# The first token tile's result goes out whole: a gated mix of a state-space convolution and a spatial-shift MLP on one core

## The chip, the cores and the metric

The kernel runs on one core of a Trainium2 chip. A core has five engines that run their own instruction lists side by side and wait for one another through semaphores: TensorE (PE; its weight loads are listed as PEld), VectorE (DVE), ScalarE (ACT), GpSimd (POOL) and SyncE (SP), which in this kernel issues nearly all DMA transfers. The metric is the device time of one execution in microseconds (us), as the median of several runs. Lower is better.

## The reference

The input `x` has 2048 tokens of 448 channels. Two branches are computed from it and mixed with a gate per token:

```python
g = sigmoid((x * gate_w).sum(-1, keepdims=True))
a = ssm_conv(x)            # long convolution per channel, plus x * D_skip
h = gelu(layernorm(x) @ w1)
hs = shift(h) @ w2         # quarters of the channels shifted by +1, -1, +2, -2 tokens
x1 = x + hs
b = x1 + gelu(layernorm(x1) @ w3) @ w4     # 448 -> 1792 -> 448
out = g * a + (1 - g) * b
```

All of it is float32.

## The kernel before

**Tiling.** The 2048 tokens are worked on in `NB` = 4 blocks of `TB` = 512, each of `NT` = 4 token tiles of 128. Tile `q` = 4 * block + place runs from 0 to 15. The tile `xs` holds the tokens in SBUF, 128 to a tile, and is overwritten in steps until it holds the result.

**Stages.** `units` lists 72 pieces of matmul work: the spatial-shift layer of all blocks, four pieces each, and then the channel MLP, 14 pieces a block. `first` (line 478) makes the hidden layer of a piece, `second` (line 602) adds its product with the second weight to the accumulators of the block's four token tiles. Float32 operands are split into a high and a low part, so each product is three matmuls. Around this, VectorE and ScalarE run the convolution branch as scans (`ssm_scan`, line 757), and SP moves turned tiles through DRAM (`xd`, `xr`, `yd`, `ysb`).

**Writing the result.** A token tile is finished when both branches have been added to it: `residual` (line 615) adds the MLP, `ssm_out` (line 787) the convolution. Each calls `done`, and the second call issues the result's transfer on SP (line 579). In block 0, tiles 0 to 3, the transfer goes out as two halves of 64 tokens each; in the other blocks as one of 128. The very last tile is written by `last_two` in two column pieces, of 320 and 128 channels (line 643).

**Lanes.** The framework that builds the program gives the transfers in turn to eight lanes, that is eight semaphores, DMAHW0 to DMAHW7; the next transfer takes the next lane, and after lane 7 comes lane 0. A transfer waits, where it isn't known already, until the one before it on its lane has landed. An instruction that needs a transfer's data waits on that transfer's lane.

**The end.** After the mixer the kernel reads a flag (line 59) and branches on it (line 60, `tc.If(ok == 0)`). With these inputs the body, `general_convolution`, is skipped. On the skipping path SP waits for its transfers, lane by lane from 0 to 7, with one wait instruction for each lane; these eight have line 60. At the program's end (line 1297) it waits once more for each lane together with one other semaphore, and then all engines meet in a barrier. The order of SP's list is that of the code as it is written; no scheduler moves it.

Of the kernel before, what the change touches and what calls it, by code (L numbers as in the profile page):

```python
# [22 lines left out]
NT = TB // 128  # L23
# [156 lines left out]
def mixer_and_small_steps(ctx, tc, xs, gg, okm, x, xT, xb, x0, w1, w2, w3, w4, gate, par, logdt, dskip, ident, out):  # L180
# [392 lines left out]
    def done(b, j):  # L573
        q = NT * b + j
        parts[q] = parts.get(q, 0) + 1
        if parts[q] == 2:
            for p in range(0, 128, 64 if b == 0 else 128):
                t = slice(p, p + (64 if b == 0 else 128))
                nc.sync.dma_start(out[q * 128 + t.start:q * 128 + t.stop], xs[t, q, :])

    ADDED = {}
# [26 lines left out]
    def residual(n, j):  # L608
        kind, b, i = units[n]
        q = NT * b + j  # L610
        r = xs[:, q, :]
        if kind == "a":
            nc.vector.tensor_add(r, ACC[j], r)
        else:
            nc.vector.scalar_tensor_tensor(r, ACC[j], gs[:, q:q + 1], r, op0=OP.mult, op1=OP.add)
            done(b, j)


    def last_two():

        n = len(units) - 2
        last = NT * NB - 1

        def add(acc, q, c):
            r = xs[:, q, c]
            nc.vector.scalar_tensor_tensor(r, acc, gs[:, q:q + 1], r, op0=OP.mult, op1=OP.add)  # L626

        add(ACC[NT - 1], last, slice(0, D))
        for j in range(NT):
            t = slice(j * 128, (j + 1) * 128)  # L630
            q = NT * (NB - 1) + j
            for c in (slice(0, D),) if q < last else (slice(0, D - 128), slice(D - 128, D)):
                acc = ACC[j] if q < last else ps.tile([128, c.stop - c.start], F32, name="p1", tag="p1", bufs=3)
                for m in (n, n + 1):
                    wh, wl = W4[units[m][2]]
                    for p in range(3):
                        nc.tensor.matmul(acc, (UL if p == 2 else UH)[m][:, t], (wl if p == 1 else wh)[:, c],  # L637
                                         start=q == last and m == n and p == 0, stop=m > n and p == 2)
                add(acc, q, c)
                if q < last:  # L640
                    done(NB - 1, j)
                else:
                    nc.sync.dma_start(out[q * 128:(q + 1) * 128, c], xs[:, q, c])
# [140 lines left out]
    def ssm_out(b, i):  # L784
        j = NT * b + i
        r = xs[:, j, :]
        nc.vector.scalar_tensor_tensor(r, YS.pop((b, i)), gg[:, j:j + 1], r, op0=OP.mult, op1=OP.add)
        done(b, i)
# [395 lines left out]
    for b in range(NB):  # L1184
        s0 = (7, 18, 31, 46)[b]
        for i in range(NT):
# [5 lines left out]
            q, when = n + (4 if b in (1, 2) else 3), late if b == 3 else before  # L1192
# [108 lines left out]
```

## Time and profile before

| what | us |
|---|---|
| median of 3 runs | 372.56 |
| lowest and highest | 371.94, 372.81 |
| profiled execution, its own time | 371.42 |
| span of that execution, first to last instruction | 369.6 |

The profile is that of one execution, whose time stands in the third row. The span is the part between its first and its last instruction, and the rest lies around it. In rows of the profile, "L579" is line 579 of the kernel, `out<-in` are the program's names, and an engine's name with a q (SPq) is its sequencer, which issues transfers, waits and branches. Times of such rows are starts from the span's beginning; durations are in ns. The closing part of the program holds these pieces of SP, by the views of their lines:

| piece | line | start, us |
|---|---|---|
| last three whole tiles issued | 579 | 361.8 to 364.3 |
| last tile's two column pieces issued | 643 | 365.0, 365.5 |
| branch | 60 | 365.9 |
| waits for the eight lanes | 60 | 367.7 to 368.2 |
| waits of the program's end | 1297 | 368.3 to 369.6 |

### The profile page before, as it was taken

What the parts mean: (1) busy time and instruction counts of PE and PEld (TensorE: products, weight loads), DVE (VectorE), ACT (ScalarE), POOL (GpSimd) and SP (SyncE); (2) the same over time, 40 slices, a digit from 0 to 9 for tenths busy, and PEclk for the clock granted to TensorE, in tenths of its full rate; (3) what the DMA queues carried; (4) which work ended last, traced back from release to release, by engine and by line L of the source; (5) the groups of instructions that cost most, each with busy time, mean ns of one, the idle gap of its engine ahead of it and who ended that gap; (6) DMA issues with size and microseconds to landing.
All of it is one profiled execution on the core that took longest, in us unless ns stands there. A gap on an engine that the chain in (4) does not pass through costs nothing.

```text
span 369.6 us, 5310 instructions
## 1 busy us (share of the span) xinstructions
PE 363.9 (98%) x1734; PEld 314.8 (85%) x1734; DVE 308.5 (83%) x571; ACT 216.1 (58%) x383; POOL 63.8 (17%) x176
## 2 busy tenths in 40 slices
PE   8999999999999999999999999999999999999995
PEld 5988888888888888888888888888888888888884
DVE  4999979788989997388789899997889999999433
ACT  5887678776674737944373774554656745445220
POOL 1000433000400000110014333324234324000000
PEclk9999999999999999999999999999999999999998
DMA  7994116727938064001833514367485611361213
GB/s 268 394 398 143 48 54 128 160 82 254 381 122 192 2 121 150 0 0 51 192 93 82 84 28 121 86 178 126 86 127 114 177 27 25 72 178 30 66 48 105
DMA packets 88495, 46.14 MB, mean 125 GB/s; under 512 B 67216, under 2 KB 82960, under 8 KB 87824
## 3 DMA queue, kind: packets, MB, share of 16 engines
q1 hardware_dynamic: 88032, 45.27, 45.5%
q10 hardware_dynamic: 432, 0.49, 0.4%
q8 instruction: 15, 0.25, 0.3%
q14 instruction: 16, 0.13, 0.1%
HBM read 34.74 MB, written 11.01 MB: 124 GB/s over the span
## 4 chain that ended last, share of the span: by engine, by line
PE 95%; DMA 3%; SPq 0%; ACT 0%; DVE 0%; issue 0%
PE p L478 48%; PE acc L602 45%; DMA raw<-x_in 2%; DMA w1r<-w_in 1%; PE acc L637 1%; PE misc L363 0%; PE p L637 0%; SPq L246 0%; ACT xh L955 0%; SPq L264 0%; DVE xs L626 0%; PE misc L734 0%
## 5 line engine op out<-in xcount | busy, mean ns | idle before, releaser
L539 ACT ACTIVATE uf<-p 128x512 f32<-128x512 f32 x56 | 33.5, 599 | 113.3 <-PE p L478 113.3
L478 PE MATMUL p<-xh,w3l 128*128 128x512 f32 x224 | 70.1, 394 | 0.0
L478 PE MATMUL p<-xh,w3h 128*128 128x512 f32 x224 | 70.0, 394 | 0.0
L757 DVE TENSOR_TENSOR_SCAN z<-z,carry 128x512 f32<-128x512 f32 x48 | 61.6, 1283 | 4.2 <-POOL z L751 0.5
L602 PE MATMUL acc<-w4l,uh 128*128 128x448 f32 x216 | 56.3, 366 | 0.0
L602 PE MATMUL acc<-w4h,uh 128*128 128x448 f32 x216 | 56.0, 365 | 0.0
L602 PE MATMUL acc<-w4h,ul 128*128 128x448 f32 x216 | 55.8, 364 | 0.0
L569 DVE TENSOR_TENSOR ul<-uf,uh 128x512 fp32r<-128x512 f32 x56 | 38.1, 681 | 20.0 <-ACT uh L549 19.8
L478 PEld LDWEIGHTS p<-xh,w3l 128*128 128x128 f32 x224 | 42.1, 188 | 9.8
L478 PEld LDWEIGHTS p<-xh,w3h 128*128 128x128 f32 x224 | 42.1, 188 | 6.6
L478 PE MATMUL p<-xl,w3h 128*128 128x512 f32 x168 | 47.7, 392 | 0.0
L602 PEld LDWEIGHTS acc<-w4h,uh 128*128 128x128 f32 x216 | 40.5, 188 | 6.0
L602 PEld LDWEIGHTS acc<-w4h,ul 128*128 128x128 f32 x216 | 40.6, 188 | 3.6
L602 PEld LDWEIGHTS acc<-w4l,uh 128*128 128x128 f32 x216 | 40.5, 188 | 3.4
L752 ACT ACTIVATE z<-zs,nu 128x512 f32<-128x512 f32 x64 | 42.3, 710 | 0.2 <-DVE xl L409 0.2
L478 PEld LDWEIGHTS p<-xl,w3h 128*128 128x128 f32 x168 | 31.5, 188 | 7.2
L549 ACT ACTIVATE uh<-uf 128x512 fp32r<-128x512 f32 x56 | 35.4, 633 | 1.8
L751 POOL COPY z<-carry 128x1 f32<-128x1 f32 x48 | 32.7, 692 | 16.0 <-DVE zs L763 15.9
L759 POOL COPY carry<-z 128x1 f32<-128x1 f32 x48 | 13.1, 273 | 105.1 <-DVE z L757 104.4
L344 POOL TENSOR_TENSOR t<-r 128x4 f32<-128x4 f32 (+1 forms) x5 | 3.1, 626 | 117.4 <-DVE r L343 117.4
L757 DVE TENSOR_TENSOR_SCAN z<-z,carry,zero 128x512 f32<-128x512 f32 x16 | 20.0, 1248 | 0.0
L602 PE MATMUL acc<-w2l,uh 128*128 128x448 f32 x64 | 19.9, 367 | 0.0
(207 smaller groups left out, 543.7 us busy)
## 6 DMA issues: line engine op xcount, KB each, us to landing
zs<-xT_in SPq DMA_DIRECT2D x4, 1024.0 KB, 8.1
yd<-yt SPq DMA_DIRECT2D x56, 64.0 KB, 2.0
ysb<-yd SPq DMA_DIRECT2D x16, 224.0 KB, 2.7
raw<-xb_in SPq DMA_DIRECT2D x3, 1032.0 KB, 12.6
raw<-w_in SPq DMA_DIRECT2D x3, 1024.0 KB, 5.6
xd<-xt SPq DMA_DIRECT2D x16, 192.0 KB, 2.1
xr<-xd SPq DMA_DIRECT2D x16, 192.0 KB, 3.1
raw<-w_in SPq DMA_DIRECT2D x3, 896.0 KB, 4.6
```

Of the source, the lines that this page charges most:

```text
L344: eng.tensor_mul(t, y, y)
L478: nc.tensor.matmul(p[:, t0:t1], (wl if w else wh)[:, k, :], (xl if x_ else xh)[:, k, o + t0:o + t1], start=(q == 0 and fresh), stop=stop i ...
L539: nc.scalar.activation(UF[n], P1[n], AF.Gelu_apprx_tanh)
L549: nc.scalar.activation(UH[n], UF[n], AF.Copy)
L569: nc.vector.tensor_sub(UL[n], uf, f32(UH[n]))
L602: nc.tensor.matmul(ACC[j], (UL if p == 2 else UH)[n][:, t], wl if p == 1 else wh, start=first_, stop=last_)
L637: nc.tensor.matmul(acc, (UL if p == 2 else UH)[m][:, t], (wl if p == 1 else wh)[:, c], start=q == last and m == n and p == 0, stop=m > n a ...
L751: nc.gpsimd.tensor_copy(z4[:, m, 0:1], carry[:, k, m:m + 1])
L752: nc.scalar.activation(z4[:, m, 1:], ZS[b][:, k, :], AF.Copy, scale=nu[:, k, m:m + 1])
L757: nc.vector.tensor_tensor_scan(z, z, up, carry[:, k, m:m + 1], OP.add, OP.add)
L759: nc.gpsimd.tensor_copy(carry[:, k, m:m + 1], z[:, TB - 1:])
```

## The change

The width of a half is now chosen by the tile's number instead of by the block. Tile 0 goes out as one transfer of 128 tokens; tiles 1 to 3 still go out in halves; all others are as they were.

```diff
         if parts[q] == 2:
-            for p in range(0, 128, 64 if b == 0 else 128):
-                t = slice(p, p + (64 if b == 0 else 128))
+            h = 64 if 0 < q < NT else 128
+            for p in range(0, 128, h):
+                t = slice(p, p + h)
                 nc.sync.dma_start(out[q * 128 + t.start:q * 128 + t.stop], xs[t, q, :])
```

One line is added, so lines behind it have a number higher by one in the changed kernel: L580 for L579, L644 for L643, L1298 for L1297.

SP's list, where the first results go out. Ahead of these rows stand two loads of `ysb`; `out_dram` is the output, "64x448" the piece, and the brackets name the semaphores that SP waits for ahead of the transfer. Before:

```order
L579 DMA out_dram<-xs 64x448 x2
L579 DMA out_dram<-xs 64x448 [waits DMAHW7_49]
L579 DMA out_dram<-xs 64x448 [waits DMAHW0_49]
L579 DMA out_dram<-xs 64x448 [waits DMAHW1_49,DVE_49]
L579 DMA out_dram<-xs 64x448 [waits DMAHW2_49]
L579 DMA out_dram<-xs 64x448 [waits DMAHW3_49,DVE_49]
L579 DMA out_dram<-xs 64x448 [waits DMAHW4_49]
L432 DMA xd<-xt 128x3x128 [waits DMAHW5_49,DVE_49]
L434 DMA xd<-xt 128x64 [waits DMAHW6_49]
```

And now, the same place:

```order
L580 DMA out_dram<-xs 128x448
L580 DMA out_dram<-xs 64x448
L580 DMA out_dram<-xs 64x448 [waits DMAHW7_49]
L580 DMA out_dram<-xs 64x448 [waits DMAHW0_49,DVE_49]
L580 DMA out_dram<-xs 64x448 [waits DMAHW1_49]
L580 DMA out_dram<-xs 64x448 [waits DMAHW2_49,DVE_49]
L580 DMA out_dram<-xs 64x448 [waits DMAHW3_49]
L432 DMA xd<-xt 128x3x128 [waits DMAHW4_49,DVE_49]
L434 DMA xd<-xt 128x64 [waits DMAHW5_49]
```

Eight transfers have become seven, the first of them whole, and from the `xd` rows on each transfer stands on the lane below the one it had.

The end of SP's list on the path that is taken. The first row's wait tells its own lane, and from there the transfers can be counted on: one lane further each. Before:

```order
L775 DMA yd<-yt 32x16x32 [waits DMAHW7_49]
L782 DMA ysb<-yd 128x448 [waits DMAHW5_49,DMAHW4_49,DMAHW6_49,DMAHW3_49,DMAHW7_49,DMAHW2_49,DMAHW0_49]
L782 DMA ysb<-yd 128x448 [waits DMAHW1_49]
L782 DMA ysb<-yd 128x448 [waits DMAHW0_49,DVE_49]
L782 DMA ysb<-yd 128x448 [waits DMAHW1_49,DVE_49]
L579 DMA out_dram<-xs 128x448 [waits DVE_49] x3
L643 DMA out_dram<-xs 128x320 [waits DVE_49]
L643 DMA out_dram<-xs 128x128 [waits DVE_49]
L60 COMPARE_AND_BRANCH
```

And now:

```order
L776 DMA yd<-yt 32x16x32 [waits DMAHW6_49]
L783 DMA ysb<-yd 128x448 [waits DMAHW5_49,DMAHW4_49,DMAHW6_49,DMAHW3_49,DMAHW7_49,DMAHW2_49,DMAHW1_49]
L783 DMA ysb<-yd 128x448 [waits DMAHW0_49]
L783 DMA ysb<-yd 128x448 [waits DMAHW7_49,DVE_49]
L783 DMA ysb<-yd 128x448 [waits DMAHW0_49,DVE_49]
L580 DMA out_dram<-xs 128x448 [waits DVE_49] x3
L644 DMA out_dram<-xs 128x320 [waits DVE_49]
L644 DMA out_dram<-xs 128x128 [waits DVE_49]
L60 COMPARE_AND_BRANCH
```

Before, the `yd` row is on lane 7, the four `ysb` rows on lanes 0 to 3, the three whole results on 4 to 6, and the two pieces of the last tile on 7 and 0. Now they are on 6, on 7 and 0 to 2, on 3 to 5, and on 6 and 7. Behind the branch, the path that is taken holds the eight waits, in this order both before and now:

```order
L60 UNCONDITIONAL_BRANCH [waits DMAHW0_49,DMAHW1_49,DMAHW2_49,DMAHW3_49,DMAHW4_49,DMAHW5_49,DMAHW6_49,DMAHW7_49]
```

The order of the instructions of the other four engines is the same as before; some of their waits name the lane below.

## The prediction

> **What bounds the kernel now.** I read the views from the coarse to the fine: the page, then the stretches, then the last five microseconds instruction by instruction. The page first.
>
> ```profile
> span 369.6 us, 5310 instructions
> PE 363.9 (98%) x1734; PEld 314.8 (85%) x1734; DVE 308.5 (83%) x571; ACT 216.1 (58%) x383; POOL 63.8 (17%) x176
> PE 95%; DMA 3%; SPq 0%; ACT 0%; DVE 0%; issue 0%
> ```
>
> TensorE (PE) is busy in 98% of the span and makes 95% of the chain that ended last. The view of busy time by stretch tells where the other 2% lie (columns: stretch, its length, then busy time of each engine with its instruction count, granted clock, DMA share, GB/s).
>
> ```profile
> 40.00:80.00 40.00, 40.00 (x190) 34.56 (x189) 34.54 (x67) 29.06 (x59) 9.98 (x32) 1.00 0.40 99
> 240.00:280.00 40.00, 40.00 (x187) 34.66 (x186) 34.48 (x46) 23.05 (x38) 12.79 (x26) 1.00 0.68 134
> 360.00:365.05 5.05, 5.04 (x30) 4.61 (x28) 3.19 (x5) 0.00 (x0) 0.00 (x0) 1.00 0.25 92
> 365.05:369.60 4.55, 0.00 (x0) 0.00 (x0) 0.35 (x1) 0.00 (x0) 0.00 (x0) 0.78 0.33 111
> ```
>
> From 40 us on PE has no gap up to 365.05 us. The second row is the stretch in which the edited transfers are issued, and PE is full there too. Then 4.55 us follow in which no matmul runs: a closing stretch of the kernel's own, and all that the end still waits for. Its pieces come from the views by source line (columns: count, shortest, median and longest duration in ns, first and last start; a last line gives the time from issue to landing). Line 643 issues the last two transfers, line 60 is the branch over the rarely used second half of the kernel with the waits behind it, line 1297 is the program's end.
>
> ```profile
> L643 SPq DMA_DIRECT2D out_dram<-xs x1: 423/423/423, 365.5 to 365.5; - x1
> DMA to landing us min/median/max: 2.2/2.2/2.2
> L60 SPq COMPARE_BRANCH  x1: 53/53/53, 365.9 to 365.9; - x1
> L60 SPq EVENT_SEMAPHORE  x1: 17/17/17, 367.7 to 367.7; - x1
> L60 SPq EVENT_SEMAPHORE  x8: 17/17/17, 367.7 to 368.2; - x8
> L60 SPq EVENT_SEMAPHORE  x1: 17/17/17, 368.2 to 368.2; - x1
> L1297 SPq EVENT_SEMAPHORE  x10: 17/28/28, 368.3 to 369.6; - x10
> ```
>
> The order is: the last transfer is issued at 365.5 us and lands 2.2 us later, at 367.7. SyncE (SP) has taken the branch at 365.9, and its first wait of line 60 starts at 367.7, with the landing. Eight such waits follow one another, one for each lane, in the order of lanes 0 to 7. Asked for 367.70 to 367.72 us the view gives the first alone (fourth row), asked for 368.24 to 368.26 the last (sixth row). Then come SP's waits of the program's end, from 368.3, and the barrier of all engines, to 369.6. In the kernel before, the last transfer signals lane 0, which is the first lane that SP waits for. So seven waits whose transfers had landed before it stand behind the one that had not.
>
> **The change part by part.** It takes one transfer from SP's list at 242 us, and so moves every later transfer by one lane; the last goes from lane 0 to lane 7.
>
> The removed transfer, and the whole one in its place:
>
> ```profile
> L579 SPq DMA_DIRECT2D out_dram<-xs x8: 466/592/605, 241.9 to 246.5; - x8
> out_dram<-xs SPq DMA_DIRECT2D x11, 224.0 KB, 2.8
> out_dram<-xs SPq DMA_DIRECT2D x8, 112.0 KB, 2.3
> L579 SPq DMA_DIRECT2D out_dram<-xs x19: 333/450/605, 241.9 to 364.3; - x19
> ```
>
> Eight halves were issued in a row at a median of 0.592 us. The whole transfers take between 0.333 us, the shortest of all 19, and 0.605, the longest; if the new one takes the median of 0.450, SP is 2 x 0.59 - 0.45 = 0.73 us earlier with what follows (bounds 0.58 to 0.85). It lands 0.5 us later than a half (2.8 against 2.3), and nothing reads `out_dram`. What follows on SP are the turned tiles of the later blocks, which reach PE through ScalarE and VectorE. The cover is that PE waits for none of them: the stretch 240 to 280 is full. I cost this at 0. From both sides: a gain cannot come, since there is no PE gap to close, and a loss needs a later arrival, while these get earlier or stay. If the cover were gone, at most these 0.73 us would show.
>
> The lanes of the transfers between 242 and 362 us: each transfer waits for the one eight places before it in the list, as before; the first few behind the edit wait for one that was issued one place earlier. No wait is added, and no instruction is put behind a new one. Also 0.
>
> The end. With the last transfer on lane 7, the waits for lanes 0 to 6 run while it is still in flight, and only one wait is left behind its landing. What goes is the distance from the first wait of line 60 to the eighth: 368.25 - 367.71 = **0.54 us**, seven steps of 77 ns. The last lanes to land set whether they do run in advance:
>
> ```profile
> L643 SPq DMA_DIRECT2D out_dram<-xs x1: 348/348/348, 365.0 to 365.0; - x1
> DMA to landing us min/median/max: 2.4/2.4/2.4
> ```
>
> The transfer before the last lands at 365.03 + 2.38 = 367.4 us, on lane 6 after the change. That leaves 0.28 us for one step of 0.08, so lane 7 is reached in time. What is late next: still the landing at 367.7, then one wait, then the end as before.
>
> A rule is weighed here. The rows give 17 ns for each wait, and starts 77 ns apart. The Trainium skill ("Perfetto Trace Analysis", section "Per-engine timelines") says that of an instruction of the sequencer the profile reports the execution alone, and neither its wait nor the time until the next is fetched. By the durations the sum would be 7 x 17 ns = 0.12 us, by the starts 0.54; the rows' starts decide, as the rule says they should.
>
> One thing the trace cannot show: when SP came to the first wait, since a wait's row begins when it is fulfilled. Bounds: as late as 367.7 (then the seven waits still run behind the landing and the gain is 0), or early, and the gain is 0.54. The nearest rows are those of the other engines behind the same branch:
>
> ```profile
> L60 DVEq COMPARE_BRANCH  x1: 76/76/76, 365.8 to 365.8; - x1
> L60 DVEq EVENT_SEMAPHORE  x1: 21/21/21, 366.4 to 366.4; - x1
> L60 ACTq COMPARE_BRANCH  x1: 45/45/45, 358.6 to 358.6; - x1
> L60 ACTq EVENT_SEMAPHORE  x1: 17/17/17, 358.8 to 358.8; - x1
> ```
>
> ScalarE took 0.2 us from the branch's start to its wait, VectorE 0.6. SP's branch at 365.9 would so bring it there by 366.1 to 366.5, at least 1.2 us ahead of the landing. Seven steps of 0.077 need 0.54. I take the early end.
>
> **The sum.** The profiled execution took 371.42 us for its span of 369.6, so 1.8 us lie around it and stay. It becomes 371.42 - 0.54 = 370.88 us, its span 369.1. That execution lies 1.1 us below the median of the runs shown (372.56, from 371.94 to 372.81), so the forecast on the runs is 372.56 - 0.54 = **372.0 us**, 0.14% less. That is below 0.2%, which is about what a measurement of this kernel can tell from no change.
>
> **The rivals.**
>
> *No gain, since SP's code is late.* Instruction packets do arrive between the branch and the landing (columns of the DMA view of 366.9 to 367.9 us: queue, packets, MB, share of 16 engines):
>
> ```profile
> q14 instruction: 2, 0.02, 8.3%
> ```
>
> 8.3% of 16 engines over 1 us are 1.33 us, 0.67 for each of two packets, all of it after 366.9; so they end between 367.6 and 367.9. If SP stood still for one of them, it came to its first wait just as the last transfer landed, the seven waits run behind it as before, and the time is 372.56. The Trainium skill ("Runtime: NRT & Kernel Launch", section "Instruction fetch mechanics") states that a taken branch whose target lies outside the two loaded pages must fetch before it can go on; by that rule the time could be this one, and no run here shows when SP resumed. Against it: VectorE, behind the same branch, ran its wait at 366.4, before both packets began, and SP's first wait starts with the landing at 365.45 + 2.24 = 367.69, which would be a coincidence. The same time would result if the waits were not walked in lane order, against which stands the program's order.
>
> *Slower: the last landing becomes late.* Transfers that are in flight while a 16 KB block of instructions is fetched land late. The four `yd` transfers issued from 336.0 to 337.4, with such a packet in the DMA view of 337.7 to 339.3, against all 56:
>
> ```profile
> q8 instruction: 1, 0.02, 5.6%
> DMA to landing us min/median/max: 1.8/3.6/3.9
> DMA to landing us min/median/max: 1.8/2.0/3.9
> ```
>
> The delay is up to 1.9 us. If the shift made the last transfer meet such a packet in full, its landing would go from 2.24 to at most 4.1 us, and the time to 372.56 - 0.54 + 1.9 = 373.9. It decides from a landing of 2.24 + 0.54 = 2.8 us: beyond it the kernel is slower than before. For it: such a packet lies near the end, in the DMA view of 363.6 to 365.1 us.
>
> ```profile
> q8 instruction: 1, 0.02, 5.4%
> ```
>
> Against it: it was there before too, under the 2.24 us that are counted. The engines' programs keep their length but for an instruction or two, so the fetches hardly move, and the last transfer's issue, which waits for PE's last product, does not move either.
>
> *More gain: the last landing gets early.* The three whole results just before landed between these bounds:
>
> ```profile
> L579 SPq DMA_DIRECT2D out_dram<-xs x3: 333/337/338, 361.8 to 364.3; - x3
> DMA to landing us min/median/max: 1.9/2.7/3.4
> ```
>
> If the last one met no delay at all, it would land in 1.9 us, 0.3 earlier than in 2.24, and the time is 372.56 - 0.54 - 0.3 = 371.7. Against it stands the same argument: nothing moves there.
>
> **How the numbers follow.** Forecast (-0.54) 0.66; no gain 0.12; early landing 0.14; late landing 0.08. The three runs shown spread by 0.87 us, so a median of such runs may stand some 0.35 us off. The bound of 0.2% is 0.75 us, only 0.2 us beyond the forecast. So about 0.3 of the forecast's 0.66, and most of the early landing's 0.14, fall under faster: 0.20 + 0.10 + 0.01 = 0.31. Slower takes about half of the late landing and a little scatter: 0.05. The rest, 0.64, is within 0.2%. The range goes from the early landing with its scatter, 371.7 - 0.4 = 371.3, to the case without gain with a part of it, 372.56 + 0.24 = 372.8.
>
> **What would show it.** Right: in the changed kernel's view of line 60, seven of SP's eight waits start before the last landing and only the eighth at it; the first wait of the program's end follows it by less than 0.1 us; from there to the span's end it is 1.3 us as before; the span is near 369.1; PE has no gap between 40 and 365 us. Wrong: all eight waits in a row behind the landing (late code), a last landing beyond 2.8 us or below 2.0 after its issue, or a new PE gap behind 242 us.

## The result and the profile after

In 19 runs of each kernel, taken in turn, the changed kernel needs 371.25 us (370.58 to 372.47) and the one before 372.04 us (371.55 to 373.17). The ratio is 0.9979, with an interval of 0.9969 to 0.9988: 0.79 us less, between 0.45 and 1.15. The forecast was 0.54 us less, from 372.56 to 372.0. The kernel is faster by a little more than forecast, and from a lower base than the three runs had shown. The profiled execution of the changed kernel took 370.7 us, that of before 371.42.

The page of the changed kernel: its span, the engines' busy time, and the shares of the chain that ended last.

```profile
span 368.9 us, 5308 instructions
PE 363.4 (99%) x1734; PEld 314.3 (85%) x1734; DVE 308.1 (84%) x571; ACT 215.9 (59%) x383; POOL 63.3 (17%) x176
PE 93%; DMA 4%; ACT 1%; DVE 0%; ACTq 0%; SPq 0%; issue 0%
```

The span is 0.7 us shorter and TensorE's work is the same, so what went is not in the work. The changed kernel's busy time by stretch (the columns are those of before):

```profile
40.00:80.00 40.00, 40.00 (x189) 34.57 (x188) 34.26 (x66) 28.67 (x57) 10.15 (x32) 1.00 0.40 99
240.00:280.00 40.00, 40.00 (x187) 34.67 (x186) 34.41 (x46) 22.86 (x38) 12.97 (x26) 1.00 0.67 134
360.00:365.05 5.05, 5.05 (x31) 4.75 (x29) 3.15 (x5) 0.00 (x0) 0.00 (x0) 1.00 0.25 91
365.05:368.92 3.87, 0.16 (x2) 0.02 (x1) 0.48 (x2) 0.00 (x0) 0.00 (x0) 0.97 0.39 131
```

TensorE is full as before, also where the edited transfers are issued. In this execution it ends 0.16 us later, and the closing stretch is 3.87 us where it was 4.55. The pieces of that stretch, by the changed kernel's views of lines 644, 60 and 1298 on SP; the first row is the edited place at 242 us:

```profile
L580 SPq DMA_DIRECT2D out_dram<-xs x7: 424/543/596, 242.1 to 246.7; - x7
L644 SPq DMA_DIRECT2D out_dram<-xs x1: 413/413/413, 365.6 to 365.6; - x1
DMA to landing us min/median/max: 1.9/1.9/1.9
L60 SPq COMPARE_BRANCH  x1: 53/53/53, 366.1 to 366.1; - x1
L60 SPq EVENT_SEMAPHORE  x7: 17/17/17, 366.6 to 367.3; - x7
L60 SPq EVENT_SEMAPHORE  x1: 17/17/17, 367.5 to 367.5; - x1
L1298 SPq EVENT_SEMAPHORE  x10: 17/28/28, 367.6 to 368.9; - x10
```

Seven of the eight waits start from 366.6 to 367.3 us, ahead of the last landing at 367.5, and one starts with it. Before, all eight stood behind the landing, from 367.7 to 368.2. And the last transfer lands 1.9 us after its issue, where it was 2.2.

The next table splits the span into three terms that add up to it, for two executions of either kernel. It is made from the starts of the same rows to 0.01 us.

| kernel | last transfer issued | issue to landing | landing to end of span | span |
|---|---|---|---|---|
| before | 365.45 | 2.24 | 1.95 | 369.64 |
| before, again (`e6_before_again`) | 365.52 | 2.21 | 1.95 | 369.68 |
| after | 365.63 | 1.88 | 1.41 | 368.92 |
| after, again (`e5_after_again`) | 365.71 | 1.89 | 1.41 | 369.01 |

The term on which the forecast rests, 0.54 us, is there to the hundredth: 1.95 - 1.41. Against the forecast stands the second term, 2.24 - 1.88 = 0.36 us, which was to stay; the first term gives 0.18 back. Whether the second belongs to the change was the question for the experiments.

### The profile page after: what moved, and what is told of

It reads as the page before. It is cut to its first block, busy times and chain, and to the rows that moved or that the text cites. A ratio compares the mean times of both kernels' runs of the same rounds, so it can differ in the third digit from the quotient of the medians.

```text
span 368.9 us, 5308 instructions
## 1 busy us (share of the span) xinstructions
PE 363.4 (99%) x1734; PEld 314.3 (85%) x1734; DVE 308.1 (84%) x571; ACT 215.9 (59%) x383; POOL 63.3 (17%) x176
## 4 chain that ended last, share of the span: by engine, by line
PE 93%; DMA 4%; ACT 1%; DVE 0%; ACTq 0%; SPq 0%; issue 0%
PE p L478 46%; PE acc L603 45%; DMA raw<-xb_in 2%; DMA xs<-x_in 2%; PE acc L638 1%; ACT xh L394 1%; PE p L638 0%; PE misc L363 0%; DVE xh L401 0%; ACT uf L996 0%; ACTq L268 0%; DVE uf L1007 0%; SPq L279 0%; ACT ug L1020 0%; ACT ug L1023 0%
```

## The experiments

Three theories. A: the lane of the last transfer is all, 0.077 us for each lane that no longer waits behind it. B, with its later form B': the change takes time out elsewhere too, in B' from the last landing. D, formed on the way: what sets the last landing is a fetch of TensorE's code, which is nothing of this change. No kernel leaves out any part of the computation. Each median stands beside one of the kernel before; kernels with the same such median (371.88, 371.70 or 371.67 us) ran in turns with it on one chip.

### Which tile, or which lane

Four kernels differ from the changed one in the choice of the tiles that go out in halves. In the first, tile 3 goes out whole in place of tile 0: the list is as long as that of the changed kernel, and the last lane is 7.

```diff
-            h = 64 if 0 < q < NT else 128
+            h = 64 if q < NT - 1 else 128
```

> Tile 3 goes out whole instead of tile 0, tiles 0 to 2 in halves; the last transfer is again on lane 7. Theory A (only the lane of the last transfer counts: one wait of about 77 ns for each lane behind it): the whole gain of seven steps, 0.54 us against the kernel before, as in the changed kernel; SP's eight waits of line 60 start before the last landing but for the last. Theory B (a part of the gain comes from what is written: the whole transfer of tile 0 lets something land or start earlier): less than the changed kernel by up to 0.3 us. Theory C (the measured 0.79 us is 0.54 us and scatter of the runs): same as A.

Measured: 371.48 us against 371.88, ratio 0.9990 (0.9979 to 1.0002). The lane's 0.54 us (0.9985) is inside this interval, and so is no gain at all. In its one profile seven waits start ahead of the landing and 1.41 us follow it, as in the changed kernel.

Next, tile 0 whole as in the change, but tile 4 in halves: the list is as long as before, and the last transfer is back on lane 0.

```diff
-            h = 64 if 0 < q < NT else 128
+            h = 64 if 0 < q <= NT else 128
```

> Tile 0 whole as in the change, but tile 4 in halves, so that the number of transfers and the lane of the last (0) are those of the kernel before. Theory A: time of the kernel before (0.0 us, within 0.2 us), all eight waits in a row behind the landing. Theory B: 0.2 to 0.3 us faster than before, since the whole transfer of tile 0 is kept.

Measured: 371.79 against 371.88, 0.9995 (0.9986 to 1.0004). Tile 0's whole transfer alone brings nothing that shows; the 0.2 to 0.3 us of theory B (0.9995 to 0.9992) lie inside the interval too, so the times alone don't exclude them. In this kernel's view of lines 644, 60 and 1298 the eight waits are behind the landing again:

```profile
L644 SPq DMA_DIRECT2D out_dram<-xs x1: 414/414/414, 365.9 to 365.9; - x1
DMA to landing us min/median/max: 1.8/1.8/1.8
L60 SPq EVENT_SEMAPHORE  x8: 17/17/17, 367.7 to 368.3; - x8
L1298 SPq EVENT_SEMAPHORE  x10: 17/28/28, 368.4 to 369.6; - x10
```

The landing was an early one, 1.8 us, on lane 0 and without the gain: a first sign that the early landing does not come with the change.

Then all tiles whole; the last lane is 4, so three waits stay behind the landing.

```diff
-            h = 64 if 0 < q < NT else 128
+            h = 128
```

> All tiles whole, four transfers fewer, the last on lane 4. Theory A: three waits are left behind the landing, so four of seven steps are gained, 0.31 us against before, less than the changed kernel. Theory B: the gain is larger than the changed kernel's, since four halves are gone instead of one.

Measured: 371.25 against 371.88, 0.9979 (0.9969 to 0.9989), 0.63 us. The rows agree with A: in this kernel's view of line 60 from 368.2 us on, four waits, that of lane 4 and three behind it.

```profile
L60 SPq EVENT_SEMAPHORE  x4: 17/17/17, 368.3 to 368.5; - x4
```

From landing to end it is 1.62 us, 0.33 less than on lane 0. The time gained more than A's 0.31 us, which is ratio 0.9992 and outside the interval; the expectation missed here.

Last, more halves instead of fewer: tiles 0 to 10, seven transfers more than before, and lane 7 again.

```diff
-            h = 64 if 0 < q < NT else 128
+            h = 64 if q < 11 else 128
```

> Tiles 0 to 10 in halves, seven transfers more than before, the last on lane 7. Theory A: 0.54 us faster than before although transfers are added. Theory B: no gain or slower, since each added half costs.

Measured: 370.86 (5 runs) against 371.88, 0.9966 (0.9952 to 0.9979): a gain with more transfers, and larger than A's 0.54 us, which is outside the interval. The profile of this kernel, by its rows of lines 580 and 60:

```profile
L580 SPq DMA_DIRECT2D out_dram<-xs x26: 332/588/602, 242.2 to 364.6; - x26
L60 SPq EVENT_SEMAPHORE  x6: 17/17/17, 366.7 to 367.1; - x6
L60 SPq EVENT_SEMAPHORE  x2: 17/17/17, 367.3 to 367.5; - x2
```

26 transfers on this line where the changed kernel has 18, and still 1.41 us from landing to end. For this stretch it is the lane, not the number of transfers nor the place of the whole one. The times don't follow the lanes as closely: `e3_all_whole` and `e4_eleven_halves` gained more than theirs, and why is open.

### The same two kernels again

> The changed kernel again, beside the kernel before on one chip, for a second interval and a second profile. Theory A (seven waits, 0.54 us, and nothing else; the rest of the first interval was scatter): 0.54 us faster, ratio 0.9985, and 1.41 us from the last landing to the span's end. Theory B (the change also lets the last transfer land earlier, by some 0.3 us): 0.8 to 0.9 us faster, ratio 0.9977, and a last landing of 1.9 us after its issue. Theory D (the last landing takes 1.8 to 2.25 us as the 16 KB of instructions fetched just ahead of it take 1.1 to 1.45 us, whatever the lane): the landing goes with that fetch's duration, below 1.9 us if it took under 1.25 us and about 2.2 if more.

> The kernel before again, as a candidate against itself: what the comparison shows where nothing differs. All theories: ratio 1 within its interval; 1.95 us from the last landing to the span's end. Theory B: a last landing of about 2.24 us again. Theory D: the landing goes with the duration of the 16 KB fetch near 364 us, as in all other profiles.

Measured: after 371.05 us against 371.70, 0.9981 (0.9970 to 0.9993); before against itself 371.75 to 371.70, 1.0009 (0.9997 to 1.0022). So a comparison of this length can be off by 0.1% by itself. A third comparison:

> The changed kernel once more, in the same call as the runs with the shorter body. Theory A with E: 0.54 us faster than before and 0.2 to 0.6 us slower than e9_short_body; its landing is 1.8 to 1.9 us if TensorE's branch takes about 3.5 us and about 2.2 if it takes 3.7 or more, and in either case 1.41 us follow the landing.

Measured: 371.04 against 371.67, 0.9982 (0.9973 to 0.9990). The three gains are 0.79, 0.65 and 0.63 us. All lie above 0.54 us, ratio 0.9985, and each interval holds it.

The traces show where one execution differs from the next. From the start of the 1500th matmul before the last, at 42 to 43 us, to the end of the last, all 18 profiles of all kernels take 322.95 to 323.01 us. So what moves TensorE's end, from 364.94 to 366.37 us, arises in the first 43 us, long before the edited place at 242 us. No gain comes from the stretch between 43 us and TensorE's end; behind it only the last issue, its landing and the closing waits are left.

### The last landing

For B' more executions were profiled, two of each kernel.

> The kernel before, one more profile. Theory B' (which of its two lengths the last landing has is settled by the program, so that the change also shortens it): 2.2 us from issue to landing, as in the two profiles of this kernel so far. Theory L (it is drawn anew in each execution): about 1.8 to 1.9 us in half of the looks. 1.95 us from landing to end in either case.

> The changed kernel, one more profile. Theory B': 1.9 to 2.0 us from issue to landing, as in its three profiles so far. Theory L: about 2.2 us in half of the looks. 1.41 us from landing to end in either case.

> The kernel before, as e13_before_look. Theory B': 2.2 us from issue to landing. Theory L: 1.8 to 1.9 us in half of the looks.

> The changed kernel, as e14_after_look. Theory B': 1.9 to 2.0 us from issue to landing. Theory L: 2.2 us in half of the looks.

The first of before, by its view of line 643:

```profile
L643 SPq DMA_DIRECT2D out_dram<-xs x1: 403/403/403, 366.8 to 366.8; - x1
DMA to landing us min/median/max: 1.8/1.8/1.8
```

And the first of the changed kernel, by its line 644:

```profile
L644 SPq DMA_DIRECT2D out_dram<-xs x1: 430/430/430, 365.9 to 365.9; - x1
DMA to landing us min/median/max: 2.2/2.2/2.2
```

These two are turned round: now before lands early and the changed kernel late. The four executions took 372.29 and 371.96 us (before) and 371.4 and 371.55 (after). Over all profiles the landing of before was 2.24, 2.21, 1.78 and 2.20 us, that of the changed kernel 1.88, 1.89, 1.99, 2.22 and 2.21. B' falls: the same program gives both landings, one in one execution and one in another. Whether the change makes the early one more frequent is not shown: it came once in four profiles of before and three times in five of the changed kernel, which is too few to tell. And the last issue itself lay between 365.45 and 366.78 us in these nine, which is a larger scatter than the effect. Landing to end was 1.95 us in every one of before and 1.41 in every one after.

### What draws the landing

TensorE's own branch of line 60 is long, and with it a 16 KB block of code arrives while transfers of the last results are in flight. Its row in the first profile of before, in the view of line 60:

```profile
L60 PEldq COMPARE_BRANCH  x1: 3727/3727/3727, 362.8 to 362.8; - x1
```

And in the first profile of the changed kernel, the same view:

```profile
L60 PEldq COMPARE_BRANCH  x1: 3467/3467/3467, 362.9 to 362.9; - x1
```

A transfer lands in sixteen parts. Part by part in the trace, fifteen parts of the last transfer have landed some 1.6 us after the issue in nearly all profiles with such a block, and one part comes 0.15 to 0.6 us later (in `e8_before_fetch_earlier` and `e10_short_body_alone`, further down, two parts are late).

In the first profile of before the block's packet runs from 363.75 to 365.04 us, so it has ended when the last transfer is issued, at 365.45. What is late is passed on. The transfer issued at 363.06 has its last part 1.44 us behind its other fifteen, the next one 0.79, and the two pieces of the last tile 0.54 and 0.60. That looks like a queue behind the block in one sixteenth of the transfers, still being worked off when the last one comes; it was not tested apart.

The landing also goes with the length of TensorE's branch. Over the fifteen profiles with the long body it was 1.78 to 1.89 us where the branch took 3.40 to 3.48 us, 1.99 at 3.55, and 2.09 to 2.58 where it took 3.73 or more. `e12_after_third` was expected to follow this, and did so to within 0.1 us. Both may have the block as their cause; that one makes the other is not shown.

D was tried by moving the code. The warm-up at the start, whose results are used nowhere, gets 2 matmuls of 512 columns and 25 of 64 in place of 7 of 512. These are 20 more, and they shift TensorE's list so that its next block falls due earlier. Once on the changed kernel, and once on before:

```diff
-    def warm_up(m):
+    def warm_up(m, cols=TB):
...
-            nc.tensor.matmul(pw, warm[:, 0:128], warm, start=True, stop=True)
+            nc.tensor.matmul(pw[:, :cols], warm[:, 0:128], warm[:, :cols], start=True, stop=True)
...
-        warm_up(7)
+        warm_up(2)
+        warm_up(25, 64)
```

> The changed kernel with the first warm-up matmuls of TensorE made more and smaller (2 of 512 columns and 25 of 64 in place of 7 of 512; their results are used nowhere), so that TensorE's list has 20 matmuls more and its 16 KB fetch near 364 us comes some 4 us earlier, near 360. Theory D: the fetch is over before the last three transfers are issued, all 16 parts of the last one land together, 1.6 to 1.7 us after its issue, and the kernel gains 0.2 to 0.6 us more than the change alone. Theory A without D: no difference from the changed kernel in the landing. If the start gets late by the longer warm-up, the last product is later by as much, and only the landing's own duration tells.

> The same warm-up in the kernel before, with the last transfer on lane 0. Theories A and D: the last landing is as short as in the run with the changed kernel (1.6 to 1.7 us), but 1.95 us follow it instead of 1.41, so it is 0.54 us slower than that run, and some 0.3 us faster than the kernel before.

Measured: 371.77 and 371.72 us against 371.70, 1.0009 (0.9998 to 1.0020) and 0.9997 (0.9986 to 1.0009). Both expectations missed. The DMA view of `e7_fetch_earlier`, first of 361 to 364 us, then of 364 to 366.5 (queue, packets, MB, share of 16 engines), and its branch:

```profile
q8 instruction: 1, 0.02, 2.0%
q8 instruction: 1, 0.02, 2.3%
L60 PEldq COMPARE_BRANCH  x1: 3832/3832/3832, 363.5 to 363.5; - x1
```

The block came earlier, at 361.7 us, but a second one came at 364.9: it starts 1.5 us after TensorE's branch and lies within it. We read this as the branch's target lying beyond what was loaded, so that the branch fetches it. The last landing was 2.09 us, and in `e8_before_fetch_earlier` 2.58. `e7_fetch_earlier` has 1.41 us from landing to end, yet no gain in time. Between these two kernels only the change differs, and by the means it is 0.08 us slower, give or take 0.5: the lane's 0.54 us does not show here. Why is open.

To test this, the skipped body itself was made shorter. Its group of channels, `GC`, goes from 8 to 2; the function computes the same, and with these inputs it is not entered. Three kernels: the change with both edits, the change with the shorter body alone, and before with both.

```diff
-GC = 8
+GC = 2
```

> The changed kernel (last transfer on lane 7) with a shorter skipped body: the convolution that line 60 skips works on groups of 2 channels instead of 8 (GC = 2), so TensorE's code in it shrinks from 160 to 40 matmuls, and with the 20 extra small warm-up matmuls. Theory E (the 16 KB fetch near 364 us is made by TensorE's own branch over the body, whose target lies beyond the code that is loaded; the fetch holds up one sixteenth of the last transfers): TensorE's branch takes under 1 us instead of 3.5 to 3.9, no 16 KB packet starts between 362.7 us and the last landing, the last part of the last transfer lands with the others, 1.6 to 1.7 us after its issue instead of 1.8 to 2.25, and 1.41 us follow it. 0.2 to 0.6 us less than the changed kernel. Theory D' (the fetch is the regular one of the next code and comes whatever is skipped): a fetch near 364 and a landing of 1.8 to 2.25 us as before.

> The changed kernel with the shorter skipped body alone, without the extra warm-ups. Theory E: TensorE's branch is short since its target is in the block loaded next, but it steps into that block, and this asks for the one after it, about 1 us earlier than the fetch before (near 363): landing between 1.6 and 1.9 us. Theory D': fetch near 364 as before.

> As e9_short_body, but with the transfers of the kernel before, the last on lane 0. All theories: 1.95 us after the last landing instead of 1.41. Theory E: with the landing out of the lottery (1.6 to 1.7 us in both), it is 0.54 us slower than e9_short_body and 0.3 to 0.6 us faster than the kernel before.

| kernel | last lane | median, us | ratio to before (371.67) | issue to landing |
|---|---|---|---|---|
| `e9_short_body` | 7 | 370.71 | 0.9977 (0.9968 to 0.9986) | 1.62 |
| `e10_short_body_alone` | 7 | 371.46 | 0.9992 (0.9980 to 1.0004) | 2.64 |
| `e11_short_body_lane0` | 0 | 371.13 | 0.9985 (0.9976 to 0.9994) | 1.63 |

In `e9_short_body` the views of line 60 and of line 644, and the DMA view of 362.5 to 367.1 us, read so:

```profile
L60 PEldq COMPARE_BRANCH  x1: 242/242/242, 362.8 to 362.8; - x1
L60 SPq EVENT_SEMAPHORE  x8: 17/17/17, 366.4 to 367.1; - x8
L644 SPq DMA_DIRECT2D out_dram<-xs x1: 404/404/404, 365.5 to 365.5; - x1
DMA to landing us min/median/max: 1.6/1.6/1.6
q14 instruction: 1, 0.01, 0.7%
```

No 16 KB block (q8) is left near the end, TensorE's branch takes 0.24 us, and the last part of the transfer lands 0.03 us behind the others. `e10_short_body_alone` tells the branch from the block. In its view of line 60, the DMA view of 364 to 366.5 us and its line 644:

```profile
L60 PEldq COMPARE_BRANCH  x1: 358/358/358, 362.7 to 362.7; - x1
q8 instruction: 1, 0.02, 2.4%
L644 SPq DMA_DIRECT2D out_dram<-xs x1: 432/432/432, 366.1 to 366.1; - x1
DMA to landing us min/median/max: 2.6/2.6/2.6
```

The branch is short here too, but a block comes at 364.8 us, under the last transfers, and they are late. It comes 27.1 us after the block before it (337.6), the distance at which the blocks of TensorE's ordinary list follow one another there, so we take it for the next of these. So a short branch does not suffice, and the block counts whatever calls for it: `e9_short_body`, whose branch is as short and which has no such block, is 0.75 us faster. In this one profile of `e10_short_body_alone` the issue is held up too: the issue of the piece before the last takes 1.16 us, where it takes 0.33 in `e9_short_body`, and so the last one starts late, at 366.1 us. The expectation of this kernel missed in part: the shorter body alone does not remove the block.

`e11_short_body_lane0`, by the last issue of its line 643 and by its view of line 60, has the early landing too, and all eight waits behind it:

```profile
DMA to landing us min/median/max: 1.6/1.6/1.6
L60 SPq EVENT_SEMAPHORE  x8: 17/17/17, 367.5 to 368.0; - x8
```

Between `e9_short_body` and `e11_short_body_lane0` only the change differs, and the late part is gone from the one profile of each. The gain is 0.42 us by the medians, 0.31 by the means, with an interval of 0.26 to either side, and 0.54 from landing to end in the profiles. It is less than the expected 0.54 us, which the interval holds. `e9_short_body` beats both kernels: 0.96 us below before, and 0.33 below the changed kernel in the same runs (`e12_after_third`, 371.04); the latter by the means is 0.31, give or take 0.30.

D's finer form, that the length of the fetch sets the landing, does not hold throughout: `e6_before_again` had a fetch of 1.18 us and landed after 2.21, the first profile after one of 1.22 and 1.88.

## Why the prediction was right or wrong

**PE as the bound, the transfer taken out at 242 us, the shift of the lanes: cost of 0 right, one reading wrong.** No gap came up between 40 and 365.05 us, and `e2_lane0_kept`, which has tile 0 whole and the old last lane, is at 0.9995. But SP is not 0.73 us earlier with what follows. Its next transfer, the first `xd`, by the views of line 432 from 247 to 248 us, before and after:

```profile
L432 SPq DMA_DIRECT2D xd<-xt x1: 538/538/538, 247.2 to 247.2; - x1
L432 SPq DMA_DIRECT2D xd<-xt x1: 532/532/532, 247.4 to 247.4; - x1
```

In both kernels it starts 5.28 us after the first result. The halves were not all issued in a row: SP waits for VectorE's tiles between them, and the time that the removed transfer freed went into the first of these waits, from 244.4 to 244.7 us before and from 243.8 to 244.9 now. That nothing showed was so for a second reason, besides PE's cover.

**The end, seven waits of 77 ns: right in mechanism and size.** 1.95 us from landing to end on lane 0, 1.62 on lane 4, 1.41 on lane 7, the same in every profile of every kernel, whichever tile went out whole and however many transfers there were. Starts, not durations, were the price.

**"I take the early end": right.** SP came to its first wait at 366.6 us, 0.45 us after its branch, and seven waits were done 0.2 us ahead of the landing. With this the rival of SP's late code falls. The rule of the Trainium skill ("Runtime: NRT & Kernel Launch", section "Instruction fetch mechanics") that a taken branch whose target is not loaded has to fetch it first was weighed for SP here; it is TensorE's branch that shows it. There the trace agrees with it: 3.4 to 4.1 us for a taken branch over the long body, with a 16 KB packet inside it, and 0.24 and 0.36 us over the short one, with none. The late landing, beyond 2.8 us, did not occur in any profile of the changed kernel.

**The landing of 2.24 us, taken as fixed: wrong.** The prediction held against an early landing that "nothing moves there". Nothing has to move: the landing differs from one execution to the next, from 1.78 to 2.24 us in kernels that are the same. The profile of before had a late one and that of the changed kernel an early one, 1.88 us, which is below 2.0 and so among the prediction's own signs of being wrong. A single profile cannot hold such a term as fixed, and the chance for an early landing, 0.14, stood for something that four of the nine profiles of the two kernels show (a landing below 2.0 us), one of before among them. It therefore belonged in the scatter. Its price was also too small. A landing without delay was put at 1.9 us, from rows of whole tiles of 224 KB; for the last piece, of 64 KB, it was 1.62 in `e9_short_body`.

**The base of 372.56 us: wrong by 0.52.** This is the step that failed most. The time of 371.25 us lies 0.05 us below the lower end of the stated range, 371.3, which was counted from this base. The prediction said that a median of three runs may be some 0.35 us off; 19 runs gave 372.04. Of the 0.77 us between the forecast (372.02) and the time, 0.52 are the base's. From 372.04 the same step gives 371.5.

The other 0.25 us, 0.79 - 0.54, is a gain beyond the lane's. It is inside the interval, and it came in all three comparisons (0.25, 0.11 and 0.09). It is not made between 43 us and TensorE's end, where every profile takes the same time to 0.06 us. What is left is the scatter of the first 43 us and of the last landing, by luck or by an early landing that the change makes more frequent; no experiment decides this, and it stays open.

**The size against 0.2%.** 0.54 us was 0.14%, and the prediction put 0.64 on a change within 0.2% and 0.31 on faster. The runs gave 0.21, 0.19 and 0.18%, which lie on both sides of the bound, and all their intervals cross it. So these runs don't tell whether the chances were well placed.

## What to carry to other kernels

Where a program's last waits are made in a fixed order, the transfer that lands last should be the last one waited for; counting the transfers behind an edit tells on which lane it comes to stand, and this was worth 0.54 us from the landing to the end, whatever the edit was for. A term read from one execution's landing counts as scatter until a second profile shows it again; for a step below 0.2%, the base needs more than three runs. Where a gain is smaller than the scatter, splitting the span into stretches tells which of them scatters and which the edit can reach. And code that is skipped can cost time at the end, by the block that is fetched while the last transfers are in flight: without it the changed kernel was 0.33 us faster by the medians, 0.31 by the means, give or take 0.30.

## What the runs showed of the hardware that was not expected

A 16 KB block of TensorE's code holds back a part of the transfers that are in flight beside it, and through them of later ones: the last landing was 1.62 and 1.63 us in the two profiles without such a block near the end, and 1.78 to 2.64 us in the sixteen with one. A taken branch on TensorE costs its sequencer 3.4 to 4.1 us where a 16 KB block is fetched within it, against 0.24 to 0.36 where none is. It does not wait for the matmuls: it started at 362.9 us in the changed kernel, 2.3 us before the last of them ended.
